# A hand-written issue order, remade behind its first third: loads, crossbars, evictions and matmul shapes

## The chip, the cores and the metric

The kernel runs on one core of one Trainium2 chip. The metric is the device time of one execution in microseconds (us). TensorE (PE in the profile) multiplies, VectorE (DVE) and ScalarE (ACT) bring results out of PSUM, GpSimd (POOL) issues the loads, and SyncE (SP) issues the crossbar transposes and the stores.

## The reference

Squared-ReLU attention over 8 batches, 12 heads, 448 positions and head size 64, then an MLP-mixer block on its result. Inputs and output are float32.

```
scores = scale * matmul(q, k.T);  attn = maximum(scores, 0)**2 / S;  x = matmul(attn, v)    # per batch and head
xt = x.transpose(0, 2, 1)                                  # x: 8 x 448 x 768
h  = maximum(xt @ w_tok1, 0) @ w_tok2                      # 448 -> 256 -> 448
u  = x + h.transpose(0, 2, 1)
out = u + maximum(u @ w_ch1, 0) @ w_ch2                    # 768 -> 1536 -> 768
```

## The kernel before

The attention is cut into 24 groups (three to a batch, four heads to a group, numbered s = 0..23), and each group's keys into 7 chunks c. What is done to a group is a set of named steps:

- `ldk`, `ldq`, `ldv` s.half (line 290, POOL): loads of 112 KB, cast to bf16, into four rotating buffers `raw_all` for each of k, q, v.
- up to s = 9, `T` s transposes k and q on TensorE; from s = 10 on, `ik`/`iq` s (line 410, DVE) copy them to `side_all`, and one crossbar transfer `x` s (line 414, SP) lands them transposed in one of three buffers `kqT_all`.
- `S` s.c (line 432, PE): four score matmuls of 64x64 weights, run side by side. `r` s.c.e (lines 268, 270) brings each half out with ReLU, `q` s.c (442, 444) squares it.
- `V` s.c (line 462, PE): four matmuls, 64x64 again, that add up the attention's result. `xe` s.half (472, 474) brings it out into `xT`.
- from s = 5 on the crossbar transfer `xd` s (line 485, SP) turns `xT` into `x_sb`; `t1` s (line 506, PE) and `t2` s (line 515) mix the positions, `u` s (line 519, DVE) adds the residual.
- `ub` b.g (line 527, SP): crossbar transfer of u for the residual of the channel part. `C1` (line 569) and `E` (line 650) are the first channel product, `c1e` its evictions; `D` (line 809) and `C2` (line 753) the second, `ds` the sums they need (line 795), `de`/`c2e` their evictions (780, 825), `st` the stores (line 727, SP; three of the last six on ACT).

T, S and V use the array as four 64x64 quarters; X, t1, t2, C1, E, D and C2 use it whole (128x128). A *change of shape* is a place where one kind follows the other on TensorE.

No scheduler orders this. The string `ORDER` holds 1928 words, one a step, and `Order.run` emits them one after the other; each engine then executes its own steps strictly in that order, with semaphores for the true dependencies. `:A` and `:D` put a step on ACT or DVE, digits name its PSUM banks. The suffix `:g` on a load or a crossbar adds a wait, a *gate*: a load so marked waits until the crossbar that stands last before it in the string has landed, a crossbar waits for the last load.

```
            if kind:
                other = last.get('cross' if kind == 'load' else 'load')
                if how == 'g' and other is not None:
                    gate(x, other)
                last[kind] = x
```

Stores are on SP too, but they are neither gated nor gates. SP and POOL each have one in-order queue, so a waiting transfer holds all behind it.

Of the kernel before, what the change touches and what calls it, by code (L numbers as in the profile page):

```python
# [111 lines left out]
V8.3 V8.4 V8.5 de1.6:D S9.4:02 V8.6 st0.64 S9.6:14 ds1.3:D xe8.1:A C1.1.8:6 ub1.4:g r9.4.0:D r9.6.0:A ik11:D xe8.0:A
r9.6.1:D t2.6.1:5 r9.4.1:A C1.1.6:0 iq11:D q9.3:D x11 u6.1:D S10.1:17 c1e1.6:A q9.0:D S10.2:42 D1.7 r10.1.1:A
r10.1.0:D r10.2.1:A iq12:D c1e1.8:A t2.6.0:5 ik12:D r10.2.0:A S9.1:07 S9.5:12 ub1.0:g ldv12.1 r9.1.0:A C1.1.5:6
r9.5.1:D r9.1.1:A u6.0:D st0.0 C1.1.2:4 q9.2:D c1e1.5:A r9.5.0:A q9.1:A t1.7.0:0 c1e1.2:D q9.6:A de1.7:D ldq16.0:g
S10.3:27 V9.0:56 rt7.0:D V9.1 ldq13.0 S10.4:14 r10.3.0:A q9.4:D D1.4 r10.3.1:A ldq16.1 ds3.1:D r10.4.1:A ldk13.0
D1.2:0 r10.4.0:A de1.4:D ldk13.1:g xd8 q9.5:A q10.4:D ldk14.0 S10.0:27 ds3.3:D V9.2 V9.3 ldv11.1:g S10.5:41 de1.2:D
V9.4 V9.5 r10.5.0:A r10.0.0:D ldk14.1:g V9.6 S10.6:30 xe9.0:A q10.3:D t2.7.0:4 ldq15.0:g r10.0.1:A D3.5:2 q10.2:D
ldq14.0 r10.6.1:A ds3.2:D q10.1:A t2.7.1:5 de3.5:D t1.8.0:7 xe9.1:A ds3.4:D r10.5.1:A xd9 D3.1:0 rt8.0:A q10.0:A D3.3
de3.1:D u7.1:D D3.2:6 de3.3:D r10.6.0:D D3.6 ik13:D q10.6:A u7.0:D ldq14.1:g t2.8.1:1 ds5.1:D q10.5:A S11.0:75 ldk16.1  # L120
de3.2:D V10.0:23 V10.1 r11.0.0:A V10.2 de3.6:D ldk15.1 S11.3:46 V10.3 r11.0.1:A u8.1:D V10.4 ldv12.0:g x12 st2.64
V10.5 r11.3.0:A V10.6 S11.5:75 ldq13.1 r11.3.1:A t2.8.0:1 r11.5.0:D xe10.1:A D3.7 u8.0:D q11.0:A S11.4:46 r11.5.1:A
de3.7:D S11.1:73 C1.2.11:1 xe10.0:D r11.1.0:A r11.4.0:A r11.4.1:D r11.1.1:A ds5.2:D S11.2:57 q11.4:A S12.0:24 S11.6:63
# [5 lines left out]
c1e2.9:A t2.9.0:7 q12.0:D D5.5:6 c1e2.4:A u9.0:D q12.3:A t2.9.1:0 de5.5:D q12.5:A S12.6:12 S13.1:43 r12.6.1:D C1.2.2:7
r12.6.0:A r13.1.0:D q12.1:A iq15:D C1.2.1:2 q12.6:D r13.1.1:A ldv13.1:g x14 ub2.0 u10.1:D D5.3 c1e2.2:D u9.1:D  # L130
S13.0:14 de5.3:D S13.2:35 V12.0:70 r13.0.1:A V12.1 r13.0.0:D V12.2 r13.2.1:A V12.3 V12.4 q13.1:D r13.2.0:A V12.5
S13.5:64 S13.3:15 V12.6 r13.5.0:A r13.3.0:D C1.2.5:3 ldv16.1 xe12.0:A xe12.1:D r13.5.1:A ldv15.1 q13.2:D t1.11.0:6
ldk15.0 c1e2.5:A ik16:D q13.0:A ldk17.0:g D5.1:1 rt11.0:D ldq17.1:g r13.3.1:A c1e2.1:D ldq17.0 S14.2:70 S13.6:43
S13.4:65 r14.2.0:D ldv13.0:g t2.11.1:2 r13.4.0:A q13.5:D D5.2:7 ldv15.0:g r13.6.1:D ldk17.1 r13.4.1:D C1.2.6:6
ldk18.0:g de5.1:D ldv14.0:g de5.2:D t2.10.0:3 c1e2.6:A t2.11.0:5 ldk18.1:g u10.0:D q13.4:A D5.6 u11.1:D r14.2.1:A
C1.2.10:7 q13.3:A de5.6:D u11.0:D q14.2:A D5.7 r13.6.0:D ub3.4 q13.6:D V13.0:63 S14.4:20 ik15:D V13.1 st4.0 c1e2.10:D
V13.2 S14.3:54 r14.4.1:A xd12 V13.3 V13.4 r14.3.1:D r14.3.0:A V13.5 S14.5:70 r14.4.0:A V13.6 S14.1:54 xe13.0:D ub2.2:g
ldq18.1 C1.3.10:2 r14.1.1:A r14.5.0:D r14.1.0:A q14.4:A r14.5.1:D C1.3.3:6 x15 xe13.1:D q14.3:A S14.0:47 q14.5:A
# [798 lines left out]
```

## Time and profile before

| | |
|---|---|
| median of 3 runs | 351.34 us (351.31 to 352.13) |
| the profiled execution, its own time | 351.98 us |
| its span | 350.2 us |
| DVE busy | 295.7 us (84%) |
| ACT busy | 227.5 us (65%) |
| POOL busy | 91.1 us (26%) |

The difference between the profiled execution's time and its span, 1.8 us, lies outside the program's first and last instruction. [...] Where the text gives a time for a step by name, it is that step's row: the page's rows name a line and tiles, and which of a line's rows it is follows from the order of the words.

### The profile page before, as it was taken

Reading aid. Unit: us, or ns where it says so; the run is one execution under the profiler, and the core shown is the slowest. Engines: PE = TensorE matmul, PEld = TensorE weight load, DVE = VectorE, ACT = ScalarE, POOL = GpSimd, SP = SyncE. Lnnn points to the kernel's source line nnn. Section 1 sums busy time; section 2 is a strip of 40 time slices with the busy share of each in tenths; the row PEclk is TensorE's granted clock in tenths of the full one; section 3 lists DMA queues with packets and bytes.
Section 4 is the critical chain, followed back from the end, with each engine's and each line's share of the span. In section 5 each row is a group of like instructions: output and inputs, shape, how many; then the busy total and the mean of one; then the engine's idle time right before and its main releaser. Section 6 shows DMA issues by size and latency. Waiting matters only on the chain.

```text
span 350.2 us, 8770 instructions
## 1 busy us (share of the span) xinstructions
PE 341.2 (97%) x3527; PEld 193.5 (55%) x3527; DVE 295.7 (84%) x581; ACT 227.5 (65%) x432; POOL 91.1 (26%) x156
## 2 busy tenths in 40 slices
PE   8999999999999999999999999999999999999994
PEld 7666556545545554555555455555555555555663
DVE  2999989997988988976898787788898999869982
ACT  3999999967588976688214554899889931334000
POOL 8883360078006420711405203021100000000000
PEclk9999999999999999999999999999999999999999
DMA  8999999999999999797999999697588330661246
GB/s 140 181 168 209 190 187 202 114 87 192 155 181 170 161 166 202 96 171 140 169 213 113 181 191 169 127 161 127 102 135 165 78 73 0 144 135 34 63 108 163
DMA packets 98121, 50.42 MB, mean 144 GB/s; under 512 B 72032, under 2 KB 94624, under 8 KB 98080
## 3 DMA queue, kind: packets, MB, share of 16 engines
q1 hardware_dynamic: 73488, 28.19, 44.0%
q0 software_dynamic: 24352, 21.47, 42.0%
q8 instruction: 27, 0.44, 0.5%
q10 hardware_dynamic: 240, 0.20, 0.2%
q14 instruction: 14, 0.11, 0.1%
HBM read 43.38 MB, written 11.01 MB: 155 GB/s over the span
## 4 chain that ended last, share of the span: by engine, by line
PE 85%; DMA 6%; ACT 3%; POOL 2%; issue 1%; DVE 1%; SPq 0%; POOLq 0%
PE w_ps L809 25%; PE m_ps L569 22%; PE sc_ps L432 9%; PE acc_ps L462 8%; PE w_ps L650 7%; PE t_ps L506 5%; PE h_ps L515 5%; POOL raw_all L290 2%; DMA raw_all<-in_v_dram 2%; DMA kqT_all<-side_all 2%; ACT sq_all L268 2%; DMA u_sb<-uT_sb 2%; PE kqT_ps L391 1%; PE m_ps L753 1%; PE x_ps L497 1%
## 5 line engine op out<-in xcount | busy, mean ns | idle before, releaser
L268 ACT ACTIVATE sq_all<-sc_ps 128x448 bf16<-128x448 f32 x217 | 108.8, 565 | 34.4 <-PE sc_ps L432 31.6
L569 PE MATMUL m_ps<-uT_sb,wc 128*128 128x448 bf16 x432 | 89.4, 353 | 0.0
L270 DVE TENSOR_SCALAR sq_all<-sc_ps 128x448 bf16<-128x448 f32 x119 | 70.7, 618 | 10.1 <-PE sc_ps L432 6.3
L442 ACT ACTIVATE sq_all<-sq_all 128x896 bf16<-128x896 bf16 x73 | 68.2, 965 | 5.6 <-DVE sq_all L270 5.3
L569 PEld LDWEIGHTS <-wc 128*128 128x128 bf16 x432 | 40.5, 98 | 40.5 <-issue 6.0
L444 DVE TENSOR_TENSOR sq_all<-sq_all 128x896 bf16<-128x896 bf16 x95 | 57.1, 617 | 0.8 <-ACT sq_all L268 0.4
L432 PE MATMUL sc_ps<-kqT_all 64*64 64x448 bf16 x672 | 55.6, 357 | 1.4 <-DMA kqT_all<-side_all 0.9
L290 POOL DMA_DIRECT2D raw_all<-in_v_dram x48 | 29.6, 623 | 91.4 <-PE sc_ps L432 30.0
L462 PE MATMUL acc_ps<-sq_all,raw_all 64*64 64x448 bf16 x672 | 45.4, 352 | 0.6 <-DMA raw_all<-in_v_dram 0.6
L809 PE MATMUL w_ps<-wd,r2d 128*128 128x384 bf16 x234 | 44.2, 327 | 0.0
L809 PEld LDWEIGHTS <-r2d 128*128 128x128 bf16 x312 | 29.6, 98 | 22.7 <-issue 2.6
L290 POOL DMA_DIRECT2D raw_all<-in_k_dram x48 | 29.6, 628 | 45.0 <-DMA kqT_all<-side_all 16.9
L268 ACT ACTIVATE r_sb<-m_ps 128x448 bf16<-128x448 f32 (+4 forms) x55 | 23.3, 461 | 20.1 <-PE m_ps L569 20.1
L780 DVE TENSOR_TENSOR out_sb<-w_ps,u_sb 128x384 f32<-128x384 f32 x52 | 28.6, 552 | 8.4 <-PE w_ps L809 7.6
L432 PEld LDWEIGHTS <-kqT_all 64*64 64x64 bf16 x672 | 22.2, 105 | 24.0 <-issue 14.6
L290 POOL DMA_DIRECT2D raw_all<-in_q_dram x46 | 28.6, 632 | 22.4 <-DVE sq_all L444 9.3
L809 PEld LDWEIGHTS <-r_sb 128*128 128x128 bf16 x234 | 22.2, 98 | 17.1 <-issue 2.6
L519 DVE TENSOR_TENSOR uT_sb<-h_ps,xT 128x448 bf16<-128x448 f32 x48 | 28.7, 617 | 1.2 <-PE h_ps L515 1.2
L809 PE MATMUL w_ps<-wc,r_sb 128*128 128x384 bf16 x156 | 29.2, 327 | 0.0
L462 PEld LDWEIGHTS <-raw_all 64*64 64x64 bf16 x672 | 20.3, 106 | 12.4 <-issue 3.3
L825 DVE TENSOR_TENSOR out_sb<-w_ps,out_sb 128x384 f32<-128x384 f32 x39 | 21.3, 552 | 5.7 <-PE w_ps L809 5.4
L506 PE MATMUL t_ps<-x_sb,wt 128*128 128x256 bf16 (+1 forms) x216 | 25.0, 261 | 0.9 <-DMA x_sb<-xT 0.9
(68 smaller groups left out, 353.5 us busy)
## 6 DMA issues: line engine op xcount, KB each, us to landing
out_dram<-out_sb SPq DMA_DIRECT2D x54, 192.0 KB, 3.0
raw_all<-in_k_dram POOLq DMA_DIRECT2D x48, 112.0 KB, 4.6
raw_all<-in_v_dram POOLq DMA_DIRECT2D x48, 112.0 KB, 4.6
raw_all<-in_q_dram POOLq DMA_DIRECT2D x46, 112.0 KB, 4.5
wc<-in_moe_w_ch_dram POOLq DMA_DIRECT2D x2, 1152.0 KB, 13.5
wc<-in_moe_w_ch_dram POOLq DMA_DIRECT2D x3, 768.0 KB, 8.6
u_sb<-uT_sb SPq DMA_TRANSPOSE x48, 2.9
side_all<-in_q_dram SPq DMA_DIRECT2D x2, 224.0 KB, 4.0
```

What stands on the lines that cost most here:

```text
L268: nc.scalar.activation(out, ps, AF.Relu)
L270: nc.vector.tensor_scalar(out=out, in0=ps, scalar1=0.0, scalar2=None, op0=ALU.max)
L290: return nc.gpsimd.dma_start(out=raws[t][s % NR][64 * half:64 * (half + 1)], in_=src[b, h0:h0 + 2].rearrange('e (p c) d -> p e (c d)', c=KC))
L432: nc.tensor.matmul(o.ps[e][64 * half:64 * (half + 1), :S], lhsT=lhsT, rhs=rhs, start=True, stop=True, skip_group_check=True)
L442: nc.scalar.activation(buf, buf, AF.Square)
L444: nc.vector.tensor_tensor(out=buf, in0=buf, in1=buf, op=ALU.mult)
L462: nc.tensor.matmul(o.ps[half][64 * e:64 * (e + 1), :S], lhsT=r[rows, e, c * D:(c + 1) * D], rhs=sq[rows, e, :], start=c == 0, stop=c == KC ...
L506: nc.tensor.matmul(o.ps[:, j, :], lhsT=wt1[:, c, j * 128:(j + 1) * 128], rhs=x_sb[:, p0:p1, c, :], start=c == 0, stop=c == 3)
L519: nc.vector.tensor_tensor(out=uTs[bb % 2][:, 2 * i + a, off:off + S].rearrange('n (c p) -> n c p', c=KC), in0=t2.ps[:, :S].rearrange('n (p ...
L569: nc.tensor.matmul(ps[:, :S], lhsT=wc1[:, g, e * 128:(e + 1) * 128], rhs=uT[:, g, off:off + S], start=g == 0, stop=g == CC - 1)
L780: nc.vector.tensor_tensor(out=out_sb[:, cols].rearrange('n (g d) -> n g d', d=128), in0=ps[:, :size].rearrange('n (g d) -> n g d', d=128), ...
L809: nc.tensor.matmul(o.ps[:, :C2], lhsT=lhs[:, e], rhs=rhs[:, e], start=holder is None and e == 0, stop=e == H2 - 1, skip_group_check=True)
```

## The change

Only the string differs. Its first 440 words stay, up to the eviction `r7.4.1` in group 7, which is 66 us into the profiled execution; the 1488 words behind it are the same steps in another sequence, some on another engine, in other banks, with other gates. Two of the lines before and two after:

```
-c1e2.11:D D3.4 r12.0.1:A r12.0.0:D q11.1:A r11.2.0:D C1.2.8:1 r11.2.1:D xd10:g ldv11.0 ldq15.1 r11.6.0:A q11.3:A
...
-V10.5 r11.3.0:A V10.6 S11.5:75 ldq13.1 r11.3.1:A t2.8.0:1 r11.5.0:D xe10.1:A D3.7 u8.0:D q11.0:A S11.4:46 r11.5.1:A
...
+xe10.1:A r12.2.0:D r12.1.0:A xd10 r12.1.1:D q11.6:A S12.4:50 V11.3 V11.4 r12.4.1:D r12.2.1:A S12.3:16 st2.0
...
+x13 C1.2.4:1 r12.3.1:D r12.6.0:A r12.5.0:D q12.1:A t1.10.0:5 st1.64 q12.5:A x14:g C1.2.2:6 rt10.0:D c1e2.4:A u9.1:D
```

Counted over the whole string: changes of shape go from 123 to 133; gates from 70 to 64; squares on ACT from 73 to 81 (so on DVE from 95 to 87); evictions `c1e` and `c2e` on ACT from 41 to 47; `r` on ACT from 217 to 213; `xe` on ACT from 33 to 35; `rt` on ACT from 19 to 21. No step is added or removed, and no PSUM or SBUF buffer. Since one line of the string is gone, all lines of code behind it have a number lower by one after the change.

**SP, around `xd10` and `x13`.** Before, from the crossbar `x12` on (line 414, into `kqT_all`); line 485 is an `xd`, line 527 a `ub`, line 727 a store. DMASW in the brackets is a wait for a load, DMAHW for an earlier transfer of SP.

```order
L414 DMA_TRANSPOSE kqT_all_72<-side_all_73 128x14x128 [waits DVE_49]
L727 DMA out_0_dram<-out_sb2_85 64x768 [waits DMAHW0_49,DVE_49]
L485 DMA_TRANSPOSE x_sb0_75<-xT1_65 128x8x128 [waits DMAHW1_49,DMASW7_49,DMAHW5_49,DVE_49,Activation_49]
L727 DMA out_0_dram<-out_sb1_84 64x768 [waits DMAHW2_49]
L727 DMA out_0_dram<-out_sb0_83 64x768 [waits DMAHW3_49,DVE_49]
L727 DMA out_0_dram<-out_sb2_85 64x768 [waits DMAHW4_49]
L414 DMA_TRANSPOSE kqT_all_72<-side_all_73 128x14x128
L727 DMA out_0_dram<-out_sb1_84 64x768 [waits DMAHW6_49]
L527 DMA_TRANSPOSE u_sb_81<-uT_sb1_80 128x3x128 [waits DMAHW7_49,DMASW1_49]
```

After, from `x12` on:

```order
L413 DMA_TRANSPOSE kqT_all_72<-side_all_73 128x14x128 [waits DVE_49]
L526 DMA_TRANSPOSE u_sb_81<-uT_sb1_80 128x3x128 [waits DMAHW0_49,DVE_49]
L726 DMA out_0_dram<-out_sb1_84 64x768 [waits DMAHW1_49]
L484 DMA_TRANSPOSE x_sb0_75<-xT1_65 128x8x128 [waits DMAHW2_49,DMAHW5_49,PE_49,Activation_49]
L726 DMA out_0_dram<-out_sb2_85 64x768 [waits DMAHW3_49]
L726 DMA out_0_dram<-out_sb2_85 64x768 [waits DMAHW4_49]
L413 DMA_TRANSPOSE kqT_all_72<-side_all_73 128x14x128 [waits DVE_49]
L726 DMA out_0_dram<-out_sb1_84 64x768 [waits DMAHW6_49]
L413 DMA_TRANSPOSE kqT_all_72<-side_all_73 128x14x128 [waits DMAHW7_49,DMASW3_49,PE_49]
```

`xd10` (the row of line 485, then 484) has lost its gate on a load (DMASW7); two stores stand between it and `x13` instead of three; `ub2.3` has come in ahead of it.

**POOL, the loads of the same stretch.** Before, from `ldk14.1` on: `ldk14.1`, `ldq15.0`, `ldq14.0`, `ldq14.1`, `ldk16.1`, `ldk15.1`, `ldv12.0`, `ldq13.1`, `ldv11.0`, `ldq15.1`.

```order
L290 DMA raw_all_71<-in_k_dram 64x2x448 [waits DMASW0_49]
L290 DMA raw_all_71<-in_q_dram 64x2x448 [waits DMASW1_49]
L290 DMA raw_all_71<-in_q_dram 64x2x448 [waits DMASW2_49]
L290 DMA raw_all_71<-in_q_dram 64x2x448 [waits DMAHW6_49,DMASW3_49]
L290 DMA raw_all_71<-in_k_dram 64x2x448 [waits DMASW4_49,DVE_49]
L290 DMA raw_all_71<-in_k_dram 64x2x448 [waits DMASW5_49]
L290 DMA raw_all_71<-in_v_dram 64x2x448 [waits DMASW6_49]
L290 DMA raw_all_71<-in_q_dram 64x2x448 [waits DMASW7_49]
L290 DMA raw_all_71<-in_v_dram 64x2x448 [waits DMASW0_49]
L290 DMA raw_all_71<-in_q_dram 64x2x448 [waits DMASW1_49]
```

After, from `ldk14.1` on: `ldk14.1`, `ldq15.0`, `ldq14.0`, `ldq14.1`, `ldv13.0`, `ldv11.0`, `ldv12.0`, `ldv14.1`, `ldv14.0`, `ldq15.1`, `ldq13.1`, `ldq18.1`.

```order
L289 DMA raw_all_71<-in_k_dram 64x2x448 [waits DMASW0_49]
L289 DMA raw_all_71<-in_q_dram 64x2x448 [waits DMASW1_49]
L289 DMA raw_all_71<-in_q_dram 64x2x448 [waits DMASW2_49]
L289 DMA raw_all_71<-in_q_dram 64x2x448 [waits DMASW3_49]
L289 DMA raw_all_71<-in_v_dram 64x2x448 [waits DMASW4_49,PE_49]
L289 DMA raw_all_71<-in_v_dram 64x2x448 [waits DMAHW7_49,DMASW5_49]
L289 DMA raw_all_71<-in_v_dram 64x2x448 [waits DMASW6_49]
L289 DMA raw_all_71<-in_v_dram 64x2x448 [waits DMAHW0_49,DMASW7_49,PE_49]
L289 DMA raw_all_71<-in_v_dram 64x2x448 [waits DMASW0_49]
L289 DMA raw_all_71<-in_q_dram 64x2x448 [waits DMASW1_49]
L289 DMA raw_all_71<-in_q_dram 64x2x448 [waits DMASW2_49]
L289 DMA raw_all_71<-in_q_dram 64x2x448 [waits DMASW3_49,DVE_49]
```

The gate of `ldq14.1` (DMAHW6, the crossbar `xd9`) is gone; the new gates are those of `ldv11.0` (`x12`) and `ldv14.1` (`ub2.3`). `ldk16.1`, `ldk15.1`, `ldk16.0` and `ldq18.0` have moved behind this stretch, `ldv13.0`, `ldv14.0` and `ldq18.1` into it.

**SP, the last stores.** Before:

```order
L727 DMA out_0_dram<-out_sb1_84 64x768
L727 DMA out_0_dram<-out_sb0_83 64x768 x2
L727 DMA out_0_dram<-out_sb1_84 64x768
L727 DMA out_0_dram<-out_sb2_85 64x768
L727 DMA out_0_dram<-out_sb3_86 64x128
L727 DMA out_0_dram<-out_sb2_85 64x768
L727 DMA out_0_dram<-out_sb3_86 64x384
L727 DMA out_0_dram<-out_sb3_86 64x256
```

After:

```order
L726 DMA out_0_dram<-out_sb1_84 64x768 x2
L726 DMA out_0_dram<-out_sb0_83 64x768
L726 DMA out_0_dram<-out_sb3_86 64x128
L726 DMA out_0_dram<-out_sb0_83 64x768
L726 DMA out_0_dram<-out_sb3_86 64x384
L726 DMA out_0_dram<-out_sb2_85 64x768 x2
L726 DMA out_0_dram<-out_sb3_86 64x256
```

The row of 64x256 is the last store of SP in both. Before, two pieces of the last tile (64x128 and 64x384) and one half of tile 26 (`out_sb2`) stand in the three places ahead of it; after, the two pieces are issued earlier, and both halves of tile 26 stand directly ahead of it.

More of the change, by code (lines that the diff above doesn't have):

```diff
@@ L129 @@
[L129 to L138, printed above, removed]
@@ new lines @@
+de3.6:D r11.3.0:A t2.8.0:3 r11.3.1:D r11.0.0:A V10.2 V10.3 u8.0:D S11.5:67 S11.4:12 V10.4 r11.5.0:D V10.5 r11.4.1:A
+V10.6 r11.5.1:A r11.4.0:D t2.8.1:3 D3.7 q11.3:A u8.1:D ldv11.0:g S11.1:62 S11.2:71 ldv12.0:g ub2.3 st1.0 r11.1.1:D
+C1.2.11:3 r11.2.0:A r11.1.0:D q11.4:A ldv14.1:g ik13:D S12.0:27 ldv14.0:g q11.1:D c1e2.11:A C1.2.9:6 ldq15.1 ds5.2:D
+r11.2.1:A r12.0.1:A ldq13.1 q11.2:D C1.2.8:3 q11.0:A de3.7:D xe10.0:A t1.9.0:1 r12.0.0:A c1e2.8:D ds5.4:D D3.4 rt9.0:A
+q11.5:D c1e2.9:A ds5.3:D S11.6:74 V11.0:23 de3.4:D S12.1:16 r11.6.1:A V11.1 V11.2 iq14:D r11.6.0:A S12.2:04 ldq18.1
```

199 lines of the change are left out of this document (102 added, 97 removed).

## The prediction

> **What bounds the kernel now.** The page comes first.
>
> ```profile
> span 350.2 us, 8770 instructions
> ...
> PE 341.2 (97%) x3527; PEld 193.5 (55%) x3527; DVE 295.7 (84%) x581; ACT 227.5 (65%) x432; POOL 91.1 (26%) x156
> ...
> PE 85%; DMA 6%; ACT 3%; POOL 2%; issue 1%; DVE 1%; SPq 0%; POOLq 0%
> ```
>
> TensorE is busy for 97% and holds 85% of the chain that ended last, and a new order takes no matmul away. So only two things can move the end by much: the few places where TensorE waits, and what it costs to arrange its work otherwise. The timeline of TensorE shows where the waits lie. First the wait of `V7.0` for `ldv7.1`:
>
> ```profile
> 78.17 0.38 PE L462 MATMUL acc_ps<-sq_all,raw_all 64*64 64x448 bf16 x2
> 79.14 0.38 PE L462 MATMUL acc_ps<-sq_all,raw_all 64*64 64x448 bf16 x2 [0.59 <-DMA raw_all<-in_v_dram]
> ```
>
> Then `t1.10.0` behind `xd10` and `S13.1` behind `x13`, with rows that price the steps:
>
> ```profile
> 120.63 0.76 PE L432 MATMUL sc_ps<-kqT_all 64*64 64x448 bf16 x12
> 121.32 1.15 PE L809 MATMUL w_ps<-wd,r_sb 128*128 128x384 bf16 x6
> ...
> 125.54 0.38 PE L432 MATMUL sc_ps<-kqT_all 64*64 64x448 bf16 x4
> 125.86 0.76 PE L462 MATMUL acc_ps<-sq_all,raw_all 64*64 64x448 bf16 x12
> ...
> 127.40 0.42 PE L462 MATMUL acc_ps<-sq_all,raw_all 64*64 64x448 bf16 x4
> 128.69 1.05 PE L506 MATMUL t_ps<-x_sb,wt 128*128 128x256 bf16 x8 [0.87 <-DMA x_sb<-xT]
> 129.58 1.30 PE L569 MATMUL m_ps<-uT_sb,wc 128*128 128x448 bf16 x6
> 130.81 0.57 PE L432 MATMUL sc_ps<-kqT_all 64*64 64x448 bf16 x8
> ...
> 132.46 0.92 PE L515 MATMUL h_ps<-wt,r_sb 128*128 128x448 bf16 x4
> 133.21 1.14 PE L809 MATMUL w_ps<-wd,r2d 128*128 128x384 bf16 x6
> 134.19 0.54 PE L515 MATMUL h_ps<-wt,r_sb 128*128 128x448 bf16 x2
> 134.66 0.38 PE L432 MATMUL sc_ps<-kqT_all 64*64 64x448 bf16 x4
> 135.89 0.38 PE L432 MATMUL sc_ps<-kqT_all 64*64 64x448 bf16 x4 [0.85 <-DMA kqT_all<-side_all]
> ...
> 139.96 1.30 PE L462 MATMUL acc_ps<-sq_all,raw_all 64*64 64x448 bf16 x24
> 141.10 0.55 PE L432 MATMUL sc_ps<-kqT_all 64*64 64x448 bf16 x8
> ...
> 149.80 1.30 PE L569 MATMUL m_ps<-uT_sb,wc 128*128 128x448 bf16 x6
> 150.93 1.14 PE L809 MATMUL w_ps<-wd,r2d 128*128 128x384 bf16 x6
> ```
>
> I read starts, not durations. Six steps of V take 141.10 - 139.96 = 1.14, so 0.19 us each; S costs the same. A first channel product takes 150.93 - 149.80 = 1.13, a second 0.98, t1 0.89, t2 0.38. With these, TensorE should have gone on at 127.40 + 0.19 + 0.1 = 127.69 and went on at 128.69: **1.00 us lost**. `S13.1` should have started at 134.85 and started at 135.89: **1.04 us**. `V11.0` should have started at 125.73, and its load `ldv11.0` let it at 125.86: **0.13 us**. At 78 it is some **0.8 us**. The same reading over the rest of the timeline finds ten or so late starts of at most 0.2 us, together about 1.
>
> **The change: the two late crossbars.** Why they were late stands in the rows of SP, POOL and the chain:
>
> ```profile
> 125.62 1.23 SPq L485 DMA_TRANSPOSE x_sb<-xT  x1
> 126.91 1.87 SPq L727 DMA_DIRECT2D out_dram<-out_sb  x3
> 128.82 2.81 SPq L414 DMA_TRANSPOSE kqT_all<-side_all  x1
> ```
>
> ```profile
> 121.40 0.61 POOL L290 DMA_DIRECT2D raw_all<-in_q_dram  x1
> ...
> 129.47 0.60 POOL L290 DMA_DIRECT2D raw_all<-in_q_dram  x1 [5.68 <-DVE side_all L410]
> 130.06 0.61 POOL L290 DMA_DIRECT2D raw_all<-in_v_dram  x1
> ```
>
> ```profile
> 128.82 7.03 DMA kqT_all<-side_all
> ```
>
> `xd10` stood gated behind `ldq13.1` (issued 121.40) and could go only at 125.62. Behind it SP issued three stores, 1.87 us, so `x13` left at 128.82; then two loads (129.47, 130.06) ran beside it and it took 7.03 us. In the new order `xd10` has no gate and waits for its own eviction alone; only `ldq18.1` can still be in flight. Between the place of `xd10` and `t1.10.0` stand four V, four S, a t2, a first channel product and three changes of shape: 8 x 0.19 + 0.38 + 1.13 + 0.3 = 3.3, with the product that is running at its place some 4.3 us. The transfer's price comes from the view of line 485, all 19 `xd`:
>
> ```profile
> DMA to landing us min/median/max: 3.0/3.3/5.8
> ```
>
> So `xd10` should land between 1.3 us ahead of need and 1.5 behind it, the latter beside many loads. I take the median, since it has one load beside it at most, and count its 1.00 us as gone.
>
> For `x13`, S12.6, three first channel products, a t1, two t2, a D and two changes stand between its place and `S13.1`: 0.19 + 3.39 + 0.89 + 0.76 + 0.98 + 0.2 = **6.4 us**. No load stands near it: the next behind `ldq18.1` is `ldk17.0`, some 10 us of TensorE's work later. The view of line 414 has all 14 such transfers:
>
> ```profile
> DMA to landing us min/median/max: 4.0/4.6/7.0
> ```
>
> At the median `x13` has 1.8 us to spare; at the longest, which is its own of before with loads beside it, it would be 0.6 late. I take the median: 1.04 us gone. `ldv11.0` now now stands four S, three first channel products of `V11.0`, so its 0.13 goes too. What is late next: `x12`, on which `ldv11.0` and `S12.0` now wait, with `ldq14.1` and `ldv13.0` ungated beside it. It has some 9 us of TensorE's work ahead of `S12.0`, against the longest row, 7.0, and 2 x 0.6 for the two loads' issues. **Sum: -2.2 us, bounds 0 and -2.2.**
>
> The wait at 78 **stays**. The sequence of POOL and SP up to `ub1.0` is the old one with its gates, so `ldv7.1` lands when it did, and TensorE reaches `V7.0` with the same work behind it.
>
> **The ten further changes of shape.** Three scores cost 121.32 - 120.63 = 0.69 where a 128x128 step follows, and 0.57 (half of 1.14) where none does: 0.12. A first channel product costs 130.81 - 129.58 = 1.23 where scores follow, against 1.13: 0.10. Ten times 0.11 is **+1.1 us**; TensorE pays it itself, and nothing hides it (bounds +1.0 and +1.2). [...] The trace bears out that a change costs, and its 0.11 us is the price here. [...]
>
> **The end.**
>
> ```profile
> 345.75 0.42 DVE L780 TENSOR_TENSOR out_sb<-m_ps,u_sb 128x256 f32<-128x256 f32 x1 [1.02 <-PE m_ps L753]
> ```
>
> ```profile
> 347.04 0.58 SPq L727 DMA_DIRECT2D out_dram<-out_sb  x1
> ```
>
> The last eviction ended at 346.17, yet its store left at 347.04, since SP was still issuing earlier ones. Now only the two stores of tile 26 stand directly ahead, and their eviction comes before the last channel product. At some 0.6 us an issue the last store can go right behind its eviction, 0.87 earlier; but two large stores are then in flight with it. I take **-0.5** (bounds 0 and -0.87).
>
> **What moves between DVE and ACT** I cost at nothing in the sum: neither is TensorE's pace-setter, and the ten small late starts will have like successors (bounds -1 and the rival's price). The cover is the slack of ACT, which gets most. Its price:
>
> ```profile
> 114.39 1.79 ACT L442 ACTIVATE sq_all<-sq_all 128x896 bf16<-128x896 bf16 x2 [1.62 <-DVE sq_all L270]
> 116.09 1.82 ACT L268 ACTIVATE sq_all<-sc_ps 128x448 bf16<-128x448 f32 x4
> ```
>
> Between `S11.0` and `V13.0` ACT had 36 short steps and 12 squares, now 40 and 16. At 0.455 and 0.895 that is 27.1 us before and 32.5 now, beside 34.9 us of TensorE's steps there, counted like the covers above: 93% full.
>
> **Sum:** 351.98 (the profiled execution) - 2.2 + 1.1 - 0.5 = 350.4, which is 1.6 less. The median before is 351.34, 0.64 under the profiled execution, so I forecast **349.8 us**.
>
> **The rivals.**
> - *A late transfer takes the old one's place.* For it: `xd10` has 4.3 us where the longest takes 5.8, and `xd12` gets a gate on a load that is issued late, `ldv15.1`. Against it: the covers of `x12` and `x13`. One wait of 1 us gives 350.8; if all waits stay, only the changes and the end count, 351.34 + 1.1 - 0.5 = 351.9. That would also be the case of a change that doesn't do what it says.
> - *ACT becomes the bound between `S11.0` and `V13.0`.* It decides when ACT's steps cannot overlap: at their mean durations (965 ns a square, 565 a short step, by the page's groups below) they need 16 x 0.965 + 40 x 0.565 = 38.0 us for 34.9, and TensorE waits 3.1 us for squares: 349.8 + 3.1 = 352.9, slower than before. For it: in-order ACT holds the `xe` of `xd10` behind all that. Against it: the two rows above, where the steps do overlap.
>
> ```profile
> L268 ACT ACTIVATE sq_all<-sc_ps 128x448 bf16<-128x448 f32 x217 | 108.8, 565 | 34.4 <-PE sc_ps L432 31.6
> ...
> L442 ACT ACTIVATE sq_all<-sq_all 128x896 bf16<-128x896 bf16 x73 | 68.2, 965 | 5.6 <-DVE sq_all L270 5.3
> ```
>
> - *More is gained:* the small late starts go as well, 349.8 - 1 = 348.8.
>
> **How the numbers follow.** The forecast has 0.57, a late transfer 0.25, ACT as the bound 0.12, the larger gain 0.06. A measurement of this kernel tells 0.3% from no change, 1.05 us: under 350.29 is faster, over 352.39 slower. Faster: 0.57 + 0.06 = 0.63; within: 0.25; slower: 0.12. The range reaches from the larger gain, 348.8, to the end of the late transfers, 351.9, and leaves out the 0.12.
>
> **What would show it.** Right: no idle time of TensorE behind `x_sb` or `kqT_all` near 128 and 135, `x13` landing in under 5 us, `V7.0` waiting as before, 133 changes of shape at 0.1 us each, the last store of SP within 0.2 us behind the last eviction. Wrong: idle rows of TensorE over 0.5 us at new places, above all `t1.10.0`, `t1.12.0` and `S12.0`; late squares between 115 and 150; changes of shape that cost nothing.

## The result and the profile after

| | before | after |
|---|---|---|
| median, 6 executions each on one chip | 351.74 us (350.53 to 356.11) | **355.25 us** (354.72 to 359.06) |
| the profiled execution, its own time | 351.98 us | 354.95 us |
| its span | 350.2 us | 353.2 us |

The change made the kernel **slower: ratio 1.011, 95% interval 1.0064 to 1.0156**. The forecast was 349.8 us. Medians here are over all executions; ratios and readings leave out those more than 1.5% above the fastest of their kernel (11 of 35 of the kernel before on one chip, none of some variants, so that a ratio can come out some tenths of a per cent above that of the medians), and with them the profiles of the runs e12 and e16 below. The same kernel differs by more between executions than the change is worth: in the whole study single executions of the kernel before took 348.34 to 358.38 us. So each run is compared with the kernel before on its own chip.

The page of the new kernel, first the lines that answer to those of before:

```profile
span 353.2 us, 8768 instructions
...
PE 343.3 (97%) x3527; PEld 192.0 (54%) x3527; DVE 290.3 (82%) x567; ACT 236.1 (67%) x446; POOL 91.1 (26%) x156
...
PE 82%; DMA 8%; ACT 3%; SPq 3%; DVE 1%; issue 1%; POOL 1%; DVEq 0%; POOLq 0%
```

ACT has 8.6 us more to do and DVE 5.4 less, as the change of engines says. In the chain, DMA has gone from 6% to 8% and SP's queue from 0% to 3%: transfers hold the end more than before. Where, the timeline of TensorE says:

```profile
75.00 1.14 PE L808 MATMUL w_ps<-wd,r2d 128*128 128x384 bf16 x6 [0.29 <-ACT sq_all L267]
...
131.98 1.05 PE L505 MATMUL t_ps<-x_sb,wt 128*128 128x256 bf16 x8 [0.56 <-DMA x_sb<-xT]
...
135.89 1.14 PE L808 MATMUL w_ps<-wc,r2d 128*128 128x384 bf16 x6
136.96 0.57 PE L431 MATMUL sc_ps<-kqT_all 64*64 64x448 bf16 x8
...
192.14 1.03 PE L431 MATMUL sc_ps<-kqT_all 64*64 64x448 bf16 x8
193.09 1.15 PE L808 MATMUL w_ps<-wc,r2d 128*128 128x384 bf16 x6
...
210.76 1.05 PE L505 MATMUL t_ps<-x_sb,wt 128*128 128x256 bf16 x8 [0.99 <-DMA x_sb<-xT]
...
225.21 0.38 PE L431 MATMUL sc_ps<-kqT_all 64*64 64x448 bf16 x3 [0.67 <-DVE out_sb L779]
...
226.58 1.05 PE L505 MATMUL t_ps<-x_sb,wt 128*128 128x256 bf16 x8 [0.43 <-DMA x_sb<-xT]
```

`S13.1` (136.96) stands right behind its predecessor: that wait is gone. `t1.10.0` (131.98) still waits for `xd10`, by 0.73 us (the first channel product ahead of it, a row that starts at 130.12, costs 1.135). And there are new places: `D1.5` (75.00), `D9.3` (193.09; the two scores ahead of it need 0.95 where 0.48 is normal), `t1.15.0` (210.76), `V17.4` behind `S18.2` (225.21), `t1.16.0` (226.58). The stretches side by side, before first (columns: stretch, its length, busy time and instructions of PE, PEld, DVE, ACT, POOL, granted clock, DMA share, GB/s):

```profile
137.00:182.00 45.00, 45.00 (x372) 24.60 (x371) 37.99 (x76) 23.24 (x45) 13.65 (x23) 1.00 0.97 159
182.00:232.00 50.00, 50.00 (x415) 27.15 (x413) 40.52 (x82) 30.45 (x56) 11.89 (x20) 1.00 0.97 158
```

After:

```profile
137.00:182.00 45.00, 45.00 (x379) 24.12 (x379) 33.00 (x66) 32.58 (x61) 11.87 (x20) 1.00 0.92 149
182.00:232.00 50.00, 47.74 (x387) 24.32 (x386) 38.08 (x77) 27.23 (x50) 13.76 (x24) 1.00 1.05 162
```

From 182 to 232 us TensorE never stopped before; now it stops for 2.3 us and starts 28 fewer matmuls. What it waits for, the chain of waits of the new kernel shows:

```profile
182.33 1.27 SPq L526
...
183.65 1.34 SPq L526
...
186.35 4.87 DMA out_dram<-out_sb
...
191.24 0.07 DVE out_sb L779
...
200.86 6.74 DMA raw_all<-in_k_dram
...
207.61 3.10 DMA x_sb<-xT
...
210.76 1.05 PE t_ps L505 x8
...
222.50 4.03 DMA x_sb<-xT
...
226.58 1.05 PE t_ps L505 x8
```

The first two rows are the issues of `ub3.1` and `ub3.5`, the next two the store `st5.64`, which stands behind them in SP's queue, and the eviction `de9.1` that waited for it. The load that took 6.74 us is `ldk22.1`, the gate of `xd15`. POOL and SP in the same stretch, new kernel (rows merge neighbours of one kind):

```profile
182.14 1.18 POOL L289 DMA_DIRECT2D raw_all<-in_q_dram  x2 [14.91 <-DVE sq_all L443]
190.55 1.18 POOL L289 DMA_DIRECT2D raw_all<-in_k_dram  x2 [7.23 <-DMA u_sb<-uT_sb]
...
200.27 1.18 POOL L289 DMA_DIRECT2D raw_all<-in_k_dram  x2
```

```profile
202.30 4.86 SPq L413 DMA_TRANSPOSE kqT_all<-side_all  x1
207.61 1.23 SPq L484 DMA_TRANSPOSE x_sb<-xT  x1
...
216.23 6.18 SPq L413 DMA_TRANSPOSE kqT_all<-side_all  x2
222.50 1.26 SPq L484 DMA_TRANSPOSE x_sb<-xT  x1
```

Read together: POOL issues `ldq22.0` and `ldq19.0` at 182.14, beside `ub3.1` and `ub3.5`, and these two crossbars then take 7.69 and 6.73 us (before: 2.53 and 3.13); `ub3.0` and `st5.64`, which SP issued behind them, land behind them, at 190.88 and 191.22. `ldk19.1` is gated on `ub3.1`, so POOL stands still for 7.23 us, and seventeen loads go in one train from 190.55 to 201.45. Before, `ldk19.1` had no gate and went at 168.17. Three things suffer. `de9.1` needs the buffer that `st5.64` empties, `de9.5` stands behind it on DVE, and so the score ahead of `D9.3` finds its bank full. `xd15`, gated on the train's last load, leaves at 207.61. And SP's work behind is late, `x19` and `xd16` among it: `iq21` on DVE waits for `x19` until 222.99, and `de11.4` stands behind it in DVE's order, so that `S18.2` finds its bank full.

**An account of the 3 us.** A row's duration overlaps the row behind it (before, the first channel product at 149.80 lasts 1.30 us, and the next row starts 1.13 later), so starts price a step. Take the prediction's costs of a step by starts, read a little finer (S and V 0.19, first channel product 1.135, second 0.975, t1 0.87, t2 0.38, a change of shape 0.10) and add them up along each kernel's own order: what an actual start is behind that sum is lateness. Between the divergence and `S13`, lateness was 3.65 us before and is 2.35 now (-1.30); from there to 181 us +0.10; from 181 to 228 us 0.56 before, **3.87** now (**+3.31**); behind that +0.41. Ten changes of shape are +0.98, an earlier start at the divergence -0.17, the end -0.32. The sum is +3.0, the difference of the spans.

### The profile page after: what moved, and what is told of

Its sections match the earlier page's. It is cut to its first block, busy times and chain, and to the rows that moved or that the text cites. A ratio compares the mean times of both kernels' runs of the same rounds, so it can differ in the third digit from the quotient of the medians.

```text
span 353.2 us, 8768 instructions
## 1 busy us (share of the span) xinstructions
PE 343.3 (97%) x3527; PEld 192.0 (54%) x3527; DVE 290.3 (82%) x567; ACT 236.1 (67%) x446; POOL 91.1 (26%) x156
## 4 chain that ended last, share of the span: by engine, by line
PE 82%; DMA 8%; ACT 3%; SPq 3%; DVE 1%; issue 1%; POOL 1%; DVEq 0%; POOLq 0%
PE w_ps L808 21%; PE m_ps L568 21%; PE sc_ps L431 9%; PE acc_ps L461 8%; PE w_ps L649 7%; PE t_ps L505 6%; PE h_ps L514 5%; DMA x_sb<-xT 3%; DMA raw_all<-in_k_dram 3%; PE m_ps L752 2%; ACT sq_all L267 2%; SPq L526 2%; PE kqT_ps L390 1%; DMA out_dram<-out_sb 1%; POOL raw_all L289 1%
## 5 line engine op out<-in xcount | busy, mean ns | idle before, releaser
L267 ACT ACTIVATE sq_all<-sc_ps 128x448 bf16<-128x448 f32 x213 | 107.6, 568 | 33.7 <-PE sc_ps L431 27.9
L269 DVE TENSOR_SCALAR sq_all<-sc_ps 128x448 bf16<-128x448 f32 x123 | 73.0, 619 | 18.3 <-PE sc_ps L431 16.9
L441 ACT ACTIVATE sq_all<-sq_all 128x896 bf16<-128x896 bf16 x81 | 75.9, 967 | 3.6 <-DVE sq_all L269 3.4
L431 PE MATMUL sc_ps<-kqT_all 64*64 64x448 bf16 x672 | 56.9, 358 | 1.4 <-DVE out_sb L779 0.7
L443 DVE TENSOR_TENSOR sq_all<-sq_all 128x896 bf16<-128x896 bf16 x87 | 52.1, 618 | 1.2 <-ACT sq_all L267 0.8
L267 ACT ACTIVATE r_sb<-m_ps 128x448 bf16<-128x448 f32 (+4 forms) x62 | 26.4, 465 | 16.8 <-PE m_ps L568 16.7
```

Of the source, the lines that this page charges most:

```text
L267: nc.scalar.activation(out, ps, AF.Relu)
L269: nc.vector.tensor_scalar(out=out, in0=ps, scalar1=0.0, scalar2=None, op0=ALU.max)
L431: nc.tensor.matmul(o.ps[e][64 * half:64 * (half + 1), :S], lhsT=lhsT, rhs=rhs, start=True, stop=True, skip_group_check=True)
L441: nc.scalar.activation(buf, buf, AF.Square)
L443: nc.vector.tensor_tensor(out=buf, in0=buf, in1=buf, op=ALU.mult)
```

## Experiments

All kernels differ from one of the two in the words of the order alone.

**e1 and e2: halves exchanged.** The string is cut near 142 us; ahead of the cut the one order, behind it the remaining words of the other.

Here the cut of e1, as a difference to the new kernel:

```diff
 u11.0:D q13.3:A ldq20.1:g D5.7 c1e2.5:D c1e2.10:A
-u11.1:D V13.0:65 S14.3:27 iq15:D V13.1
+st4.64 ub2.1:g iq15:D ldv16.1 ldv15.1
...
```

> The new order up to c1e2.10 (some 141 us), then every word that is left in the old order. Theory (the loss lies behind 142 us, in transfers that come late from 182 us on): TensorE starts the old rest about 0.9 us earlier than in the kernel before (waits up to there 2.0 for 3.1, an earlier start at the divergence by 0.18, four more changes at 0.1), so 0.5 to 1.2 us faster than before. Rival (the new order costs evenly, by its ten changes of shape and by ACT, which has its heaviest stretch here): as slow as before or up to 1.5 us slower.

> The old order up to ub3.4 (some 142 us), then every word that is left in the new order. Theory (loss behind 142 us): 3.5 to 4.5 us slower than before, thus slower than the new kernel too, with t1.15.0 behind xd15 by about 1.2 us, V17.4 by 0.8, t1.16.0 by 0.7, D9.3 by 0.5. Rival (an even cost of changes and ACT): only six more changes are in this half, 0.6 us slower than before.

Measured: e1 357.67 us against 351.96 of before (ratio 1.0198, 1.0145 to 1.0251), e2 359.57 (1.0235, 1.018 to 1.029). Both are slower, so the times tell nothing of halves: the seam itself costs, 7.7 us of lateness between 142 and 181 in each, probably since steps that each order had done by then are missing. Part of it was run at half the clock, behind waits of 3.1 and 3.5 us: the granted clock was 0.50 from 154.8 to 158 us in e1 and from 166 to 172.5 in e2. The profiles do tell: behind 181 us, e1 (old order) is late by 0.67 us. e2 (new order) is late by 0.61 there too; TensorE arrived 7 us late, and the transfers were in time. So the new order's loss at 181 to 228 is a race between transfers and TensorE, not a cost of its steps.

**e3 to e6: the tail's causes, one by one.** Each is the new kernel with one edit. e3:

```diff
-r16.0.1:D ldq22.0:g ub3.1 r15.5.1:A ldq19.0 q15.2:A
+r16.0.1:D ub3.1 r15.5.1:A q15.2:A
...
-ldk19.1:g ub3.5 r16.3.0:A
+ldk19.1:g ub3.5 ldq22.0:g ldq19.0 r16.3.0:A
```

> The new kernel, with ldq22.0 and ldq19.0 moved from beside ub3.1 to behind ub3.5. Theory (these two loads slow ub3.1 and ub3.5, ub3.1 holds ldk19.1 and the fifteen loads behind it, the last of them holds xd15): ub3.1 takes 3 to 4.5 us for 7.7, ldk19.1 is issued at 185 to 187 for 190.55, xd15 before 205 for 207.6, and the waits at D9.3, t1.15.0, V17.4 and t1.16.0 (3.1 us in sum) mostly go: 2 to 3 us faster than the new kernel. Rival (TensorE is late there for its banks, and the transfers only fill the same holes): within 0.5 us of the new kernel.

Measured: 355.46 us, ratio 1.0132 (1.0081 to 1.0183), no gain. The cause was right: `ub3.1` took 4.9 us and `ldk19.1` left at 186.21. (The train has sixteen loads behind `ldk19.1`, not fifteen.) But `ldq19.0`, moved behind them, landed at 191.81, `iq19` on DVE waited for it, and `de9.1` and `de9.5` stand behind `iq19`: `D9.3` was 2.5 us late, and from 196 to 198 us the granted clock was 0.50. The edit had made its own late load; e5 avoids it:

```diff
-ldq19.1 C1.3.3:3
+ldq19.1 ldq19.0 C1.3.3:3
...
-r16.0.1:D ldq22.0:g ub3.1 r15.5.1:A ldq19.0 q15.2:A
+r16.0.1:D ub3.1 r15.5.1:A q15.2:A
...
-ldk19.1:g ub3.5 r16.3.0:A
+ldk19.1:g ub3.5 ldq22.0:g r16.3.0:A
```

> The new kernel, with ldq22.0 behind ub3.5 (gated) and ldq19.0 far ahead, behind ldq19.1, so that it cannot be late itself. Theory: ub3.1 and ub3.5 take 3 to 5 us each, ldk19.1 goes at 186 or 187 for 190.55, its train ends near 203 for 207.6, xd15 is issued near 204.5, x19 near 213 for 216.2; the waits at D9.3, t1.15.0, S18.5, V17.4 and t1.16.0 (3.4 us in sum) go but for some 0.7: 2 to 3 us faster than the new kernel. Rival (these waits are taken up by others wherever they are removed, since SP, DVE and the banks have no slack left there): under 0.7 us faster.

Measured: 354.39 us against 353.32 of before, **ratio 1.0032 (0.9987 to 1.0077)**, where the new kernel has 1.011. The new kernel's median lay 3.5 us above that of before, e5's lies 1.1 above: two moved loads give back about 2.4 us. POOL, SP and TensorE in e5:

```profile
188.82 0.59 POOL L289 DMA_DIRECT2D raw_all<-in_k_dram  x1 [20.09 <-DMA u_sb<-uT_sb]
...
199.77 1.35 POOL L289 DMA_DIRECT2D raw_all<-in_k_dram  x2
```

```profile
203.71 2.53 SPq L413 DMA_TRANSPOSE kqT_all<-side_all  x1
206.34 2.31 SPq L484 DMA_TRANSPOSE x_sb<-xT  x1
```

```profile
209.86 1.30 PE L568 MATMUL m_ps<-uT_sb,wc 128*128 128x448 bf16 x6
211.00 1.04 PE L505 MATMUL t_ps<-x_sb,wt 128*128 128x256 bf16 x8
```

`x18` leaves 2.6 us behind the train's last issue, not 0.85, and holds SP for 2.53 us, not 4.86; `t1.15.0` (211.00) follows its predecessor without a stop. `D9.3` (0.35), `V17.4` (0.84) and `t1.16.0` (0.25) stay, against the expectation: `st5.64` landed at 192.61, where `de9.1` waited for it, and `x19`, issued at 216.36 and not 213, still came late for `iq21`.

e6 takes the gate from `xd15`:

```diff
-C1.4.7:6 xd15:g c1e4.5:D
+C1.4.7:6 xd15 c1e4.5:D
```

> The new kernel, with xd15 ungated alone. Theory: xd15 is issued near 204.5 for 207.6, beside the last loads, takes 4 to 5 us and lands by 209.5, so t1.15.0's 1.16 us goes; SP is 2 to 3 us earlier behind it, so x19 lands by 220.5 and the waits at S18.5 and V17.4 (1.1 us) go; D9.3 keeps its 0.5: 1.5 to 2.3 us faster than the new kernel. Rival: xd15 beside loads takes 6 to 8 us, and nothing is gained.

Measured: 357.81 us against 353.32, ratio 1.0086 (1.0043 to 1.013): the rival. The gate was not what held `xd15`. SP of e6:

```profile
206.09 5.32 SPq L413 DMA_TRANSPOSE kqT_all<-side_all  x1
211.46 1.31 SPq L484 DMA_TRANSPOSE x_sb<-xT  x1
```

`xd15` waits for nothing now and still leaves 5.37 us after `x18`, because the issue of `x18` itself held SP for 5.32 us (2.53 in e5, where it began 2.6 us behind the train's last issue). So my reading of the chain was wrong in one link: its "gate" was a wait that would have been there anyway.

**e4: the loads ahead of `xd10`.**

```diff
-q11.4:A ldv14.1:g ik13:D
+q11.4:A ik13:D
...
-xd11 r12.6.1:A
+xd11 ldv14.1:g ldv14.0 ldq15.1 ldq18.1 r12.6.1:A
```

> The new kernel, with ldv14.1, ldv14.0, ldq15.1 and ldq18.1 moved from ahead of xd10 to behind xd11, the first of them gated on it. Theory (loads in flight lengthen a crossbar): xd10 takes 3.0 to 3.6 us for 4.9, t1.10.0's wait of 0.73 us goes, and the end comes 0.3 to 0.8 us earlier than the new kernel's. Rival (xd10 is slow for the stores st2.0 and st2.64 and for x13 behind it): 4.5 us and more, no change of the time.

Measured: `xd10` took 3.1 us, for 4.90 in the new kernel, with the stores still beside it, and `t1.10.0` has no wait: the loads in flight had lengthened it. Yet 355.67 us, ratio 1.0154 (1.0084 to 1.0224): no gain. `ldv13.1`, `ldk15.0` and others behind the moved four came later, and around 152 to 156 us `V13.0` and `C1.3.10` waited for 1.4 us more than in the new kernel.

**e7: the three edits together** (e5, e6, and three of e4's loads behind `ldk16.0`).

> The new kernel with the edits of the two runs above together, and ldv14.1, ldv14.0 and ldq18.1 moved from ahead of xd10 to behind ldk16.0 (ldq15.1 stays, so that iq15 is not late). Theory: xd10 takes 3.0 to 3.6 us and t1.10.0's 0.73 goes as well: 3 to 4 us faster than the new kernel, as fast as the kernel before or up to 1 us faster. Rival (removed waits come back elsewhere): under 1.5 us faster than the new kernel, slower than before.

Measured: **353.20 us against 353.32 of before, ratio 1.0037 (0.9994 to 1.008)**; lateness up to `S13` 1.61 and from 181 to 228 us 2.03. By the medians it is 3.6 us faster than the new kernel, as the theory has it, by the ratios 2.6. `xd10` took 3.07 us, and the waits at `t1.10.0`, `D9.3`, `t1.15.0` and `t1.16.0` are gone. Those at `S18.5` (0.52) and `V17.4` (0.84) stay, although `x19` left 3.1 us earlier than in the new kernel: beside two loads issued at 210.77 and 211.56 it took 7.77 us. So here these two waits come from `x19`'s own slowness, not from the train.

**e8: the price of a change of shape.** The kernel before, with 21 swaps such as this one:

```diff
-S18.1:71 S17.4:35 r17.5.1:D D11.3 de11.1:D
+S18.1:71 D11.3 S17.4:35 r17.5.1:D de11.1:D
```

> The kernel before, with one S or V swapped with its 128x128 neighbour at 21 places between 100 and 275 us whose operands and banks are ready: 42 more changes of shape, 165 in all, nothing else. Theory (0.10 us a change): 4.1 us slower, with late starts of 0.2 us around each swapped step. [...]

Measured: 356.59 us against 353.32, **ratio 1.0102 (1.0064 to 1.0141)**: 3.6 us for 42 changes, 0.09 us each (0.05 to 0.12). TensorE of e8, single steps of S between second channel products:

```profile
216.12 0.38 PE L432 MATMUL sc_ps<-kqT_all 64*64 64x448 bf16 x4
216.43 1.15 PE L809 MATMUL w_ps<-wc,r2d 128*128 128x384 bf16 x6
217.51 0.38 PE L432 MATMUL sc_ps<-kqT_all 64*64 64x448 bf16 x4
```

From one S to the next 217.51 - 216.12 = 1.39 us; a product takes 0.975 and an S 0.19, so two changes cost 0.22, 0.11 each. The expected 0.10 a change lies within the range that the times give.

**e9 to e11: the new kernel again, its banks, and all edits.** e10, to which belongs that banks 0 and 2 change places from `D1.5` on:

```diff
-q7.1:A D1.5:2 c2e0.0.1:D r8.1.1:A
+q7.1:A c2e0.0.1:D D1.5:0 r8.1.1:A
...
-V7.2 r8.3.0:A
+V7.2 c1e1.1:A r8.3.0:A
...
-S12.1:16 r11.6.1:A V11.1
+S12.1:16 r11.6.0:A r11.6.1:A V11.1
...
-V17.0:25 de11.4:D V17.1
+V17.0:05 de11.4:D iq21:D ik21:D V17.1
```

> The new kernel itself, for the comparison on this chip and for a second profile. Theory: 3 to 4 us slower than before again, and the waits that hang on the order come back with their sizes: D1.5 0.4, D1.3 0.4, D5.5 0.2, V17.4 0.8, t2.16.1 0.2, and t1.15.0 and t1.16.0 by 0.5 to 1.2 each; the wait at S8.3 (0 to 2 us in the profiles so far, of both orders) varies with the landing of wc2.1. Rival: the waits lie elsewhere in each execution, and the loss is not to be put down to places.

> The new kernel; no load, crossbar or PE step moves. c2e0.0.1's word stands ahead of D1.5 again, so that D1.5 can have bank 0 (banks 0 and 2 change places from there on); ACT does c1e1.1 ahead of r8.3.0 and r11.6.0 ahead of r11.6.1; DVE does iq21 and ik21 behind de11.4. Theory (part of the loss is evictions that hold a bank, not transfers): the waits at D1.5 (0.37), D1.3 (0.38), D5.5 (0.21), S18.5 (0.26) and V17.4 (0.84) go; up to t1.10.0 0.2 to 1.0 us are gained, but t1.16.0 behind xd16 takes over what S18.5 and V17.4 leave: 0.5 to 1.5 us faster than the new kernel. Rival (transfers alone set the time): under 0.3 us.

> The new kernel with all edits so far: ldq22.0 behind ub3.5, ldq19.0 behind ldq19.1, xd15 ungated, ldv14.1, ldv14.0 and ldq18.1 behind ldk16.0, the edits of engines and banks of the run beside this one, and xd16 ahead of x20. Theory: the waits that hang on the order fall from some 5.5 us to under 1; 4 to 5 us faster than the new kernel, 0.5 to 2 us faster than before: the gain that the prediction saw, less nothing for the ten changes, which stay. Rival (each removed wait shows another): no faster than before.

Measured, against 352.88 of before on this chip: e9 356.25 us (ratio 1.0131, 1.0065 to 1.0197), e10 355.72 (1.0129, 1.0085 to 1.0173), **e11 352.12 (1.003, 0.9985 to 1.0075)**. In e9 the same places came back: `D1.5` 0.37, `D1.3` 0.45, `t1.10.0` 1.24, `D9.3` 0.28, `t1.15.0` 2.60, `V17.4` 0.84, `t1.16.0` 0.68. So they belong to the order, though their sizes vary. e10 took away the waits for banks at `D1.5` and `V17.4`, halved that at `D1.3` and lengthened, by its swap, that at `D5.5` to 0.51. It gained nothing that can be measured, with `t1.15.0` late by 2.19; that fits the rival, transfers set the time, but the two intervals would hide a gain of 1 or 2 us. TensorE at `t1.15.0`, in e9 and then in e11:

```profile
210.31 1.31 PE L568 MATMUL m_ps<-uT_sb,wc 128*128 128x448 bf16 x6
214.05 1.05 PE L505 MATMUL t_ps<-x_sb,wt 128*128 128x256 bf16 x8 [2.43 <-DMA x_sb<-xT]
```

```profile
207.71 1.30 PE L568 MATMUL m_ps<-uT_sb,wc 128*128 128x448 bf16 x6
208.86 1.04 PE L505 MATMUL t_ps<-x_sb,wt 128*128 128x256 bf16 x8
```

e11 is 4.1 us faster than e9, as expected, and 3.6 faster than e10, from which only the transfers set it apart; but it is not faster than the kernel before, against the expectation of 0.5 to 2.

**e12 to e16: the gain that the prediction counted on.** e12 mends the two late crossbars of the kernel before and nothing else; e13 to e15 move `ldv7.1` (the wait at 78 us) in the old, the new and the mended new order; e16 is e12 with that move and `ldv11.0` ahead of `ldv12.0`. e12:

```diff
-r11.2.1:D xd10:g ldv11.0
+r11.2.1:D xd10 ldv11.0
...
-x13 V11.5
+x13 st1.64 st4.64 st2.0 V11.5
```

The move of `ldv7.1`, as e13 has it:

```diff
-ldv7.0:g xd5
+ldv7.0:g ldv7.1 xd5
```

> The kernel before, with only the two late crossbars mended: xd10 ungated, and the stores st1.64, st4.64 and st2.0 moved from ahead of x13 to behind it. The prediction's first step by itself: the waits of t1.10.0 (1.00) and S13.1 (1.04) go and nothing takes their place, no change of shape is added: 1.5 to 2.1 us faster than before. Rival (another late transfer or S8.3's wait takes over): within 0.7 us of before.

> The kernel before, with ldv7.1 moved from behind ldq10.1 to right behind ldv7.0, nothing else. Theory (ldv7.1 stands behind ldk9.0, which is gated on a crossbar that is late when the last startup weights, wc2.1, are late; it landed between 75.4 and 81.8 us in the profiles and TensorE needs it at 77.6): ldv7.1 lands by 73, no wait at V7.0 or S8.3, 0.5 to 1.5 us faster in the median. Rival: ub0.0 or the loads behind it come later by the move and hold D1 or t1.6.0 instead: no change.

> The new kernel, with the same move of ldv7.1. Theory (V7.0's wait is the same in both orders, and the order's own loss lies at D1.5, D1.3, t1.10.0 and from D9.3 to t1.16.0): 0.5 to 1 us faster than the new kernel, and 3 to 4 us slower than the kernel before with the same move. Rival (the wait at 78 us, not the order, makes the difference): as fast as that one.

> The new kernel with all its mended places (the run e11_all_fixes, with r11.6.1 ahead of r11.6.0 again, since that swap made D5.5 wait 0.5 for 0.2) and the move of ldv7.1. Theory: waits that hang on the order under 1.2 us; 1 us faster than e11, so 1 to 2 us faster than before. Rival: other late transfers take over; as fast as before.

> The kernel before with xd10 ungated, st1.64, st4.64 and st2.0 behind x13 (as in e12), ldv11.0 ahead of ldv12.0, and the move of ldv7.1. Theory (the two crossbars' 2.0 us were real, and V11.0 behind ldv11.0 took them over in e12): no wait over 0.3 us at V7.0, V11.0, t1.10.0 and S13.1, 2 to 3 us faster than before. Rival: under 1 us.

| run | median | before there | ratio (95%) |
|---|---|---|---|
| e12 | 352.18 us | 352.88 us | 1.0001 (0.9963 to 1.0039) |
| e13 | 352.48 us | 353.56 us | 0.9977 (0.9934 to 1.0021) |
| e14 | 356.34 us | 353.56 us | 1.0132 (1.0078 to 1.0186) |
| e15 | 353.41 us | 353.56 us | 1.0043 (1.0003 to 1.0082) |
| e16 | 355.31 us | 353.56 us | 1.0029 (0.9978 to 1.0079) |

e14 bore out the half of its theory that matters here: with `ldv7.1` moved in both, the new order is still 3.9 us slower than the old. The gain of 0.5 to 1 us on the new kernel can't be seen (ratio 1.0132, that of e9 was 1.0131). e12, e15 and e16 went to the rivals: none gained what the removed waits had measured. e13 decides nothing, its 1.1 us by the medians lie within its interval, 2.3 us faster to 0.7 slower; but its profile shows how a removed wait can be lost. TensorE there:

```profile
86.43 0.38 PE L462 MATMUL acc_ps<-sq_all,raw_all 64*64 64x448 bf16 x4 [0.52 <-DMA raw_all<-in_v_dram]
...
92.31 1.05 PE L506 MATMUL t_ps<-x_sb,wt 128*128 128x256 bf16 x8 [0.51 <-DMA x_sb<-xT]
...
99.86 0.57 PE L432 MATMUL sc_ps<-kqT_all 64*64 64x448 bf16 x8 [0.95 <-DMA kqT_all<-side_all]
...
129.81 1.05 PE L506 MATMUL t_ps<-x_sb,wt 128*128 128x256 bf16 x8
...
135.78 0.82 PE L432 MATMUL sc_ps<-kqT_all 64*64 64x448 bf16 x8
```

`V7.0` no longer waits, but `V8.0`, `t1.6.0` and `x10`'s first score do, and `t1.10.0` and `S13.1`, which had cost 2.04 us in the profile before, cost 0.14 and 0.24. My reading: all loads behind 67 us stand in one queue whose start varies; a wait taken out early is met again later, and TensorE that has waited early finds the later transfers landed. Lateness in the two stretches, by profile, in us (the stretches have the same steps in every kernel of an order, so their times shift a little):

| kernel | 66 us to `S13` | 181 to 228 us |
|---|---|---|
| before; e8; e13 (old order) | 3.65; 4.41; 4.31 | 0.56; 0.51; 0.58 |
| after; e9 (new order) | 2.35; 4.34 | 3.87; 4.94 |
| e4; e6; e10; e14 (new, other edits) | 2.44; 5.31; 2.32; 5.07 | 2.98; 3.81; 4.42; 2.24 |
| e5; e7 (tail's loads mended) | 3.31; 1.61 | 1.96; 2.03 |
| e11; e15 (all mended) | 1.40; 3.95 | 0.77; 0.48 |

The left column varies from execution to execution in both orders (e1 and e3 have 1.6 and 1.7 there, e2 3.6); the right one separates them. e3 has 5.2 in it, by the late load of its own.

## Why the prediction was wrong

It had the wrong sign. Its terms stood for -1.6 us, the profiles differ by +3.0.

- **The step that failed: "the ten small late starts will have like successors"**, that is, nothing but ten changes of shape and the last stores happens behind 137 us. There the new order adds 3.31 us of lateness. I followed the queues of POOL and SP to `x13` and left the 1093 words behind almost unread for gates, though the same reading would have found it: a load newly gated on `ub3.1`, two loads beside that crossbar, sixteen behind the gate. e5, e7 and e11 show this cause: with the transfers there moved, the ratio falls from 1.011 or 1.013 to 1.003 or 1.004. About 1.1 of the 3.3 us, at `S18.5` and `V17.4`, hang on DVE's order besides: they stay in e7 and went in e10 and e11, where DVE does `iq21` behind `de11.4`.
- **The two late crossbars: a term that was mis-sized.** `S13.1` and `V11.0` went as said; `t1.10.0` went from 1.00 to 0.73, since `xd10` met four loads and took 4.90 us, not the median 3.3 ("it has one load beside it at most" was wrong; it was so in e3 alone, where `xd10` took 3.71 us and nothing waited). Worse, most of the 2.2 us was one execution's: at the same two steps e2, whose words are the old ones up to 142 us, waits 0.23 and 0.32 us, and e13 0.14 and 0.24; and mending them alone (e12) gave no measurable gain. The stretch gained 1.3 us in the profiled pair; over all profiles read here its lateness is 1.4 to 5.3 us in the new order and its variants, 3.6 to 4.4 in the old.
- **The wait at 78 stays:** in the profile after it is gone, in e9 it was 1.15 us. It hangs on when `ldv7.1` lands, 75.4 to 81.8 us in the profiles read here that leave it in its place, of both orders, so that the profiled pair gained 0.78 us there was luck.
- **What moves between DVE and ACT costs nothing:** not quite. The new places of evictions and banks brought `D1.5` 0.36 and `D1.3` 0.38 behind ACT's evictions, `D5.5` 0.21, and a part in the 0.84 at `V17.4`; what these are worth in time, e10 is too coarse to tell. ACT did not become the bound: from `S11.0` to `V13.0`, the rival's stretch, it was busy for 32.6 us, as the prediction had added up (32.5), of 36.3, and TensorE waited there for `xd10` and hardly for anything else.
- **Ten changes of shape, +1.1:** right, by e8's 0.09 to 0.11 each. (The account's 0.98 shows nothing more, since it puts in 0.10 a change.)
- **The end, -0.5:** right in kind. In the new kernel, DVE and SP at the end:

```profile
349.08 0.42 DVE L779 TENSOR_TENSOR out_sb<-m_ps,u_sb 128x256 f32<-128x256 f32 x1 [0.75 <-PE m_ps L752]
```

```profile
342.85 7.50 SPq L726 DMA_DIRECT2D out_dram<-out_sb  x9
```

  The last eviction ends at 349.50 and SP's last issue at 350.35, so at 0.6 us an issue it began 0.3 behind the eviction and not 0.87, 0.6 earlier; the span has 0.32 of that.
- **The rivals:** "a late transfer takes the old one's place" was the right kind with too small a price. I let it cost one wait, or give back the gain, in the stretch that I had read, and named `t1.10.0`, `t1.12.0` and `S12.0`. It had to be allowed to lose more than the change gains, anywhere in 280 us of new order. The 0.3% that a measurement was to tell from no change was too fine as well: the interval came out at 0.46% either way.

That the mended order e11 is no faster than the old one follows from the same account: its profile has 3.15 us of lateness in sum for 4.55, but ten changes cost 1.0 and it came 0.3 later to the divergence, so its last step of TensorE starts at 344.14 us, and that of before at 344.24. The 1.003 that is left by the ratio, 1.1 us, is about the price of the ten changes. Left open is what decides when the last startup weights, `wc2.1`, land (63.5 to 66.3 us in the profiles read here). That the loads behind 67 us start from there, and with them the lateness of the left column, is a reading that no run tests.

## What to carry to other kernels

When an order is remade, read every gate and every queue to the end of the program, not to the last wait that the change is meant to remove: here the new gate of `ldk19.1` held POOL for 7.23 us, and `x18`, 0.85 us behind the last issue of the seventeen loads that followed in one train, held SP for 4.86 us. Where waits come from transfers, look at two or three profiles before pricing one: in the old order the waits at `t1.10.0` and `S13.1` were 2.04 us in the profile before and 0.38 in e13, while the lateness up to `S13` was 3.65 and 4.31; in the new order that sum varied too, 2.35 and 4.34. A wait removed early can be met later: e13, rid of the one at `V7.0`, met 0.52, 0.51 and 0.95 us behind it. And look for the loads that run beside a crossbar, and for when the last of them lands, before giving it its median: `xd10` was given 3.3 us and took 4.90.

## What the runs showed of the hardware

- **Crossbar transfers beside loads took longer, and held SP's queue.** `xd10` took 3.06 to 3.08 us in the four profiles of the new order's variants in which no load was in flight beside it (e4, e7, e11, e15), and 3.7 to 5.4 in the eight with one to five loads. In each of these eight it landed 0.8 to 1.1 us behind the last of the loads, so its time followed the last landing; in the kernel before, where three loads ended in its first 1.35 us, it took 3.03. `ub3.1` took 2.5 us in the kernel before, 7.3 to 8.0 beside the two loads in the new order (5.4 in e2) and 4.5 to 4.9 where they are moved away; why not 2.5 stays open. The issue of `x18` held SP for 2.53 us in e5, where it began 2.6 us behind the train's last issue, and for 4.86 in the new kernel, 0.85 behind it. So nearer to POOL's loads the issue on SP's queue took longer as well.
- **Behind waits of some 2 us TensorE's clock was halved in two of three profiles.** In e10, after 2.02 us of idle time, `D11.5` (212.33) took 2.06 us from start to start; in the new kernel the same step took 1.07 (211.64 to 212.71). TensorE, then the windows (the last three numbers: granted clock, DMA share, GB/s):

```profile
211.44 1.09 PE L505 MATMUL t_ps<-x_sb,wt 128*128 128x256 bf16 x8 [2.02 <-DMA x_sb<-xT]
212.33 2.13 PE L808 MATMUL w_ps<-wd,r2d 128*128 128x384 bf16 x6
```

```profile
213.00:214.50 1.50, 1.50 (x9) 0.54 (x11) 0.80 (x2) 0.00 (x0) 0.00 (x0) 0.50 1.13 194
...
216.00:218.00 2.00, 2.00 (x14) 1.09 (x12) 1.48 (x4) 0.54 (x1) 0.41 (x1) 1.00 0.86 175
```

  In e3 the clock fell to 0.50 as well, after 2.13 us of idle time at 191.8; in e9 it stayed at 1.00 after 2.43 us at the place of e10, so two of the three profiles with an idle time of 2.0 to 2.5 us have the fall. What sets it off, no run shows.
